# Three moves at the seam between the attention stage and the expert stage: a subtraction's source, six transposes, three gate instructions

## The chip, the cores and the metric

The kernel runs on one core of one Trainium2 chip. Its time is the device time of one execution in microseconds; less is better. Times of single instructions come from one profiled execution, whose span runs from the first to the last instruction.

## The reference

Three layers run one after the other, all in float32:

```python
for t in range(S):                                  # attention: B 4, H 8, S 768, D 48
    state = alpha[:, :, t, :, None] * state + einsum('bhd,bhe->bhde', k[:, :, t], v[:, :, t])
    y[:, :, t] = einsum('bhd,bhde->bhe', q[:, :, t], state)
x = y.transpose(0, 2, 1, 3).reshape(B * S, H * D)   # 3072 rows of 384
do = x @ w_skip > 0                                 # experts: only rows with a positive skip score
e_idx = argmax(x @ w_gate); gate = softmax(x @ w_gate)[e_idx]
x[do] += gate * (relu(x[do] @ w1[e_idx]) @ w2[e_idx])     # 8 experts, 384 -> 1024 -> 384
h = maximum(maximum(x @ m1, x @ m2), x @ m3)        # last layer: 384 -> 768 -> 384
out = h @ m_out
```

## The kernel before, in words

**Attention.** The work is cut into 24 steps: 4 batches (`b`) of 6 chunks (`c`) of 128 positions. Step `n` computes the scores of step n+1 (`scores`, L246), the transposes of its keys (`trans`, L237), the rows of the step before (`rows`, L297: four products that turn the attention output `yt` into 128 rows of 384 plus nine routing scores, in the PSUM tile `px`), then its own output (`outs`, L284 and L287, in `py`, copied to `yt` by L290) and the state's update (`upd`, L264; L271 and L272 on VectorE and the two copies L275 and L276 into `bd`, which the next step's `outs` reads). ScalarE copies `px` to `xr` in SBUF (L311). For the last four chunks it also writes the rounded high part `xq[0]` (L310), and `low_part` (L315, VectorE) writes the low part `xq[1]`, the difference between the row and its high part. For chunks 0 and 1 of the last batch `xsplit` does the same from `xr` (L99, L100).

**Routing.** `route` is a generator that gives every row a slot of its expert (256 slots each); `stage` runs it to its next stop. For batches 0 to 2 it covers six chunks. The last batch is cut in two: `rA` (chunks 0 to 3) and `rB` (chunks 4 and 5). A route computes the expert (L339 to L358), sends the rows to the row table `x2` in HBM (L361), counts with two products (L365, L366), forms the slot number (L371 to L381) and, in the last batch, the one-hot tiles `p0` (L384). Then come the gates (L392 to L394: sum, plus 1e-9, reciprocal) and one indirect DMA from GpSimd's queue for each chunk (L397), which writes the rows with their gates into `slots` in HBM.

**The first expert's input.** Expert 0 doesn't wait for the last batch's rows to go through HBM. The tile `xe` is loaded from `slots` after the scatters of batches 0 to 2 (L512, SyncE's queue). The last batch's rows are added by products: `gather` (L522) multiplies `xq` with `p0` into three PSUM accumulators `acc`, one for each third of the 384 columns, and six transposes (L540, weights `xe`, moving operand `ident`) add the rows that came through `xe`. `split` then forms `xh` and `xl` of expert 0 (L99, L100).

**Experts.** 64 slices `s`: `gemm1(s)` (L624 to L626) and, two slices later, `gemm2` (L642 to L644). The input of expert 1 is loaded with `xload(1)` (L599) once all scatters have landed, and TensorE transposes it from slice 5 on (`xprep`, L612). After the experts the last layer runs 36 groups of products (L778 to L780, L810 to L812).

**What sets the order.** The kernel is recorded with a manual schedule: each engine runs its instructions in the order in which the code issues them, and semaphores hold an instruction until its inputs are there. An instruction that waits holds everything behind it on its engine.

Of the kernel before, what the change touches and what calls it, by code (L numbers as in the profile page):

```python
# [9 lines left out]
F32 = mybir.dt.float32  # L10
# [5 lines left out]
ALU = mybir.AluOpType  # L16
# [4 lines left out]
NP = H // 2  # L21
C = 128
NC = S // C
PR = 128
# [6 lines left out]
DM = H * D  # L31
# [3 lines left out]
CAP = 256  # L35
# [28 lines left out]
def tile_gla_moe_moe2(ctx, tc, akq, vp, rp, wgt, cst, io, ew, md, out):  # L64
    nc = tc.nc
    V, A, G, T, SY = nc.vector, nc.scalar, nc.gpsimd, nc.tensor, nc.sync
# [6 lines left out]
    k3, nf1, nf2 = DM // 128, FF // 128, FF2 // 128  # L73
# [24 lines left out]
    def split(h, l, src, eng=None):  # L98
        A.copy(h, src)  # L99
        (eng or V).tensor_tensor(l, src, h.bitcast(F32), ALU.subtract)  # L100

    with tc.manual_schedule():
        cs = const.tile([128, 3 * 128 + NTILE + 8], F32, name="cs")
        rps = const.tile([PR, NP, 105], F32, name="rps")
        ident = cs[:, 0:128]
# [14 lines left out]
        xq = []  # L120
# [12 lines left out]
        ps_s = pool("ps_s", 1, space=PSUM)  # L133
        ps_k = pool("ps_k", 1, space=PSUM)
        ps_u = pool("ps_u", 1, space=PSUM)
# [28 lines left out]
        def warm(n):  # L164
            pw = ps_r.tile([128, 512], F32, name="pr")
            for i in range(n):
                T.matmul(pw, ones, wu, start=True, stop=True)
# [4 lines left out]
        nseq = len(seq)  # L172
# [13 lines left out]
        def vload(j):  # L186
            if j >= nseq:
                return
            b, c = seq[j]
            vt[j] = hp.tile([128, VW], F32, name="vt")  # L190
            SY.dma_start(out=vt[j], in_=vp[b, :, c])
# [32 lines left out]
        def prep(j):  # L224
            if j < nseq:
                sf = suffixes(j)
                inverse(j, sf)
                prefixes(j, sf)

        fr, kks, yts, wt, xr, lg = {}, {}, {}, {}, {}, {}  # L230

        def trans(j):
            if seq[j][1] == NC - 1:
                return
            pk = ps_k.tile([128, NP, PR], F32, name="pk")
            for p in range(NP):
                T.transpose(pk[:, p, :], kh[j][:, p, :], ident)  # L237
            kks[j] = wk.tile([128, NP, PR], F32, name="kk")
            A.copy(kks[j], pk)

        def scores(j):
            ps = [ps_s.tile([128, NP, C], F32, name=f"ps{i}") for i in range(2)]
            for p in range(NP):
                for i in range(2):
                    r0 = 64 * i
                    T.matmul(ps[i][:, p, :], kh[j][r0:r0 + 64, p, :], qh[j][r0:r0 + 64, p, :],  # L246
                             start=True, stop=True)
            fr[j] = ps

        def mask(j, i):  # L250
            t = wk.tile([128, NP, C], F32, name=f"sm{i}")
            V.tensor_tensor(t, fr[j][i], cmask[:, None, :].to_broadcast([128, NP, C]), ALU.mult)
            fr[j][i] = t
# [24 lines left out]
        def outs(j):  # L278
            c = seq[j][1]
            sm = fr.pop(j)  # L280
            py = ps_y.tile([PR, NP, C], F32, name="py")
            if c:
                for p in range(NP):
                    T.matmul(py[:, p, :], bd[c % 2][:, p, :], qh[j][:, p, :], start=(p == 0), stop=False)  # L284
            for p in range(NP):
                for i in range(2):
                    T.matmul(py[64 * i:64 * i + 64, p, :], vt[j][:, (2 * p + i) * D:(2 * p + i) * D + 64], sm[i][:, p, :],  # L287
                             start=(c == 0), stop=(c == 0 or p == NP - 1))
            yts[j] = wk.tile([PR, NP, C], F32, name="yt")
            A.copy(yts[j], py)  # L290

        def rows(j):
            b, c = seq[j]
            yt = yts.pop(j)
            px = ps_x.tile([128, NP, 105], F32, name="px")
            for p in range(NP):
                T.matmul(px[:, p, :], yt[:, p, :], rps[:, p, :], start=True, stop=True)  # L297
            if c == 0:
                xr[b] = wk.tile([128, NC, XW], F32, name="xr")
                lg[b] = cols[f"lg{b % 2}"].rearrange("p (c e) -> p c e", c=NC)  # L300
            pairs = lambda t: t.rearrange("p (a d) -> p a d", a=NP)
            direct = b == B - 1 and c > 1

            def logits():
                V.tensor_reduce(lg[b][:, c, :], px[:, :, 96:105].rearrange("p a e -> p e a"), AX.X, ALU.add)

            if direct:
                if c == NC - 1:
                    logits()
                A.copy(pairs(xq[0][:, c]), px[:, :, 0:96])  # L310
            A.copy(pairs(xr[b][:, c, 0:DM]), px[:, :, 0:96])  # L311
            if not direct or c < NC - 1:
                logits()
            def low_part():
                V.tensor_tensor(pairs(xq[1][:, c]), px[:, :, 0:96], pairs(xq[0][:, c]).bitcast(F32), ALU.subtract)  # L315

            return low_part

# [132 lines left out]
        def stage(*gs):  # L451

            gs = list(gs)
            while gs:
                gs = [g for g in gs if next(g, 1) == 0]

        def step_routes():
            for r in routes:
                stage(r)

        def xsplit(c0, c1, eng=None):
            z = slice(c0, c1)
            split(xq[0][:, z], xq[1][:, z], xr[B - 1][:, z, 0:DM], eng)

        scores(0)
        trans(0)
        prep(1)
# [2 lines left out]
        for n, (b, c) in enumerate(seq):  # L470
            pre = [n + 2] if n == 0 else [n + 2, n + 3] if n == 1 else [n + 3]
            pre = [j for j in pre if j < nseq]
            if n + 1 < nseq:
                scores(n + 1)
                trans(n + 1)
            for j in pre:
                prep(j)
            if n + 1 < nseq:
                mask(n + 1, 0)
                mask(n + 1, 1)  # L480
            low_part = rows(n - 1) if n else None
            outs(n)
            upd(n)
            if n > nseq - 4:
                low_part()
            vload(n + 5)
            if n and seq[n - 1][1] == NC - 1:
                routes.append(route(b - 1, 0, NC))
            step_routes()
            if n < 2:  # L490
                warm(KEEP[n])
            if n == 3:
                patterns()
            if n == 10:
                SY.dma_start(out=iota, in_=io)
            if 3 <= n < 7:
                for i in range((n - 3) * NSLOT // 512, (n - 2) * NSLOT // 512):
                    SY.dma_start(out=slots[i * 128:(i + 1) * 128, :], in_=zt)
            if 7 <= n < 11:
                wpart(n - 7)  # L500
            if n in (11, 12, 13, 18):
                wsplit(min(n - 11, 3), G)
            if n in (17, 18):
                wload(n - 16)
            if n == nseq - 4:
                rs.close()
                xep = xes.enter_context(tc.tile_pool(name="xep", bufs=1, side="right"))
                xq += [xep.tile([128, NC, DM], F32R, name=f"xq{i}") for i in range(2)]
                p0 = xep.tile([128, NC, CAP], F32R, name="p0")
                xe = xep.tile([128, 2, DM], F32, name="xe")  # L510
            if n == nseq - 3:
                SY.dma_start(out=xe, in_=slots[0:CAP, 0:DM].rearrange("(m p) d -> p m d", p=128))  # L512
            if n == nseq - 2:
                rA = route(B - 1, 0, 4)
                stage(rA)
                xsplit(0, 2)

        def gather(c0, c1):
            for c in range(c0, c1):
                for k in range(k3):  # L520
                    for t in xq:
                        T.matmul(acc[k], t[:, c, k * 128:(k + 1) * 128], p0[:, c], start=(c == 0 and t is xq[0]),  # L522
                                 stop=(c == NC - 1 and t is xq[1]))

        stage(rA)
        stage(rA)
        low_part = rows(nseq - 1)
        rB = route(B - 1, 4, NC)
        stage(rB)
        low_part()  # L530
        acc = [ps_k.tile([128, NP, PR], F32, name="pk").rearrange("p a b -> p (a b)")[:, 0:CAP],
               ps_u.tile([128, 512], F32, name="pu")[:, 0:CAP],
               ps_s.tile([128, NP, C], F32, name="ps0").rearrange("p a b -> p (a b)")[:, 0:CAP]]
        gather(0, 3)
        stage(rB)
        stage(rA)
        gather(3, 4)
        for k in range(k3):
            for m in range(2):
                T.matmul(acc[k][:, m * 128:(m + 1) * 128], xe[:, m, k * 128:(k + 1) * 128], ident,  # L540
                         start=False, stop=False)
        stage(rB)
        gather(4, NC)
        stage(rB)
        xs_, xh_, xl_, ix_ = {}, {}, {}, {}
        xh_[0] = xhp.tile([128, k3, CAP], F32R, name="xh")
# [493 lines left out]
```

## Time and profile before

| | |
|---|---|
| median of 3 runs | 614.12 us (614.08 to 615.0) |
| the profiled execution's own time | 614.44 us |
| its span, first to last instruction | 612.6 us |
| time around the span | 1.84 us |
| TensorE busy | 585.9 us, 96% |
| VectorE, ScalarE, GpSimd busy | 359.8, 239.7, 161.7 us |
| mean granted TensorE clock | 0.994 of 2.4 GHz |

The attention stage runs up to about 139 us, the seam between the stages from there to 146 us, the experts to about 303 us, the last layer to the end. TensorE is the engine that is nearly always busy, so the rows to look for are those in which it waits. In a timeline a row has the start, the duration, the engine, the line, the operation, the tile written and the tile read, the shape, how many instructions were merged into the row, and in brackets how long the engine was idle before it and what ended that. PE is TensorE's matmul, PEld its weight load, DVE is VectorE, ACT ScalarE, POOL GpSimd, SPq the DMA queue of SyncE.

### The profile page before, as it was taken

What the parts mean: (1) busy time and instruction counts of PE and PEld (TensorE: products, weight loads), DVE (VectorE), ACT (ScalarE), POOL (GpSimd) and SP (SyncE); (2) the same over time, 40 slices, a digit from 0 to 9 for tenths busy, and PEclk for the clock granted to TensorE, in tenths of its full rate; (3) what the DMA queues carried; (4) which work ended last, traced back from release to release, by engine and by line L of the source; (5) the groups of instructions that cost most, each with busy time, mean ns of one, the idle gap of its engine ahead of it and who ended that gap; (6) DMA issues with size and microseconds to landing.
All of it is one profiled execution on the core that took longest, in us unless ns stands there. A gap on an engine that the chain in (4) does not pass through costs nothing.

```text
span 612.6 us, 10428 instructions
## 1 busy us (share of the span) xinstructions
PE 585.9 (96%) x4103; PEld 525.8 (86%) x4103; DVE 359.8 (59%) x630; ACT 239.7 (39%) x495; POOL 161.7 (26%) x142
## 2 busy tenths in 40 slices
PE   5999999989999999999999999999999999999994
PEld 3888888889998999999888888888888888888884
DVE  5899999966889899998577223222322322332222
ACT  2555575654666666654333121121121212112111
POOL 5544598744256455455100000000000000000000
PEclk9999999999999999999999999999999999999998
DMA  8789998925777767673241030020003001001001
GB/s 326 263 236 340 294 309 304 364 63 184 256 281 250 244 230 259 231 282 121 73 169 38 1 103 1 1 99 6 0 1 103 1 1 51 1 0 52 0 2 57
DMA packets 29243, 85.67 MB, mean 140 GB/s; under 512 B 3298, under 2 KB 20688, under 8 KB 27264
## 3 DMA queue, kind: packets, MB, share of 16 engines
q1 hardware_dynamic: 26336, 79.68, 37.7%
q0 software_dynamic: 2560, 4.83, 2.1%
q8 instruction: 34, 0.56, 0.4%
q10 hardware_dynamic: 288, 0.39, 0.2%
q14 instruction: 25, 0.20, 0.1%
HBM read 67.47 MB, written 20.49 MB: 144 GB/s over the span
## 4 chain that ended last, share of the span: by engine, by line


## 5 line engine op out<-in xcount | busy, mean ns | idle before, releaser
L795 DVE TENSOR_TENSOR h<-ph,h 128x512 f32<-128x512 f32 x72 | 49.8, 691 | 157.8 <-PE ph L780 157.4
L778 PE MATMUL ph<-xh,mh 128*128 128x512 f32 x270 | 106.3, 394 | 0.0
L780 PE MATMUL ph<-xh,ml 128*128 128x512 f32 x270 | 105.6, 391 | 0.0
L779 PE MATMUL ph<-xl,mh 128*128 128x512 f32 x270 | 105.4, 390 | 0.0
L99 ACT CAST hh<-h 128x512 fp32r<-128x512 f32 x36 | 22.3, 620 | 143.2 <-DVE h L795 143.2
L100 POOL TENSOR_TENSOR wl<-raw,wh 128x768 fp32r<-128x768 f32 x26 | 50.4, 1938 | 57.2 <-ACT wh L99 54.5
L100 DVE TENSOR_TENSOR wl<-raw,wh 128x768 fp32r<-128x768 f32 x38 | 58.0, 1526 | 11.2 <-ACT wh L99 11.2
L99 ACT CAST wh<-raw 128x768 fp32r<-128x768 f32 x64 | 53.4, 834 | 20.8 <-PE po L644 16.6
L780 PEld LDWEIGHTS ph<-xh,ml 128*128 128x128 f32 x270 | 50.7, 188 | 10.9
L779 PEld LDWEIGHTS ph<-xl,mh 128*128 128x128 f32 x270 | 50.7, 188 | 9.9
L778 PEld LDWEIGHTS ph<-xh,mh 128*128 128x128 f32 x270 | 50.7, 188 | 9.8
L624 PE MATMUL ph<-xh,wh 128*128 128x256 f32 x192 | 56.4, 294 | 1.5 <-DVE hl L630 1.5
L625 PE MATMUL ph<-xl,wh 128*128 128x256 f32 x192 | 54.4, 283 | 0.4 <-DVE xl L100 0.3
L626 PE MATMUL ph<-xh,wl 128*128 128x256 f32 x192 | 54.3, 283 | 0.0
L812 PE MATMUL po<-mh,hl 128*128 128x384 f32 x144 | 48.6, 338 | 0.0
L810 PE MATMUL po<-mh,hh 128*128 128x384 f32 x144 | 48.4, 336 | 0.0
L811 PE MATMUL po<-ml,hh 128*128 128x384 f32 x144 | 48.4, 336 | 0.0
L793 ACT COPY h<-ph 128x512 f32<-128x512 f32 x36 | 21.1, 586 | 68.0 <-PE ph L780 68.0
L644 PE MATMUL po<-wh,hl 128*128 128x384 f32 x128 | 43.6, 340 | 1.7 <-DVE hl L630 1.3
L642 PE MATMUL po<-wh,hh 128*128 128x384 f32 x128 | 43.5, 340 | 0.0
L643 PE MATMUL po<-wl,hh 128*128 128x384 f32 x128 | 43.1, 337 | 0.0
L246 PE MATMUL ps<-q,k 64*128 64x128 f32 x384 | 31.9, 287 | 11.0 <-POOL q L221 7.1
(188 smaller groups left out, 1188.2 us busy)
## 6 DMA issues: line engine op xcount, KB each, us to landing
raw<-in_ew_dram SPq DMA_DIRECT2D x15, 1536.0 KB, 6.4
akq<-in_akq_dram SPq DMA_DIRECT2D x23, 772.5 KB, 7.0
rm<-in_md_dram SPq DMA_DIRECT2D x12, 768.0 KB, 7.7
vt<-in_vp_dram SPq DMA_DIRECT2D x24, 200.0 KB, 7.2
out_dram<-o SPq DMA_DIRECT2D x22, 192.0 KB, 2.0
xg<-x SPq DMA_DIRECT2D x5, 768.0 KB, 5.3
x<-xr SPq DMA_DIRECT2D x3, 1152.0 KB, 10.1
slots<-zt SPq DMA_DIRECT2D x16, 193.0 KB, 7.3
```

Of the source, the lines that this page charges most:

```text
L99: A.copy(h, src)
L100: (eng or V).tensor_tensor(l, src, h.bitcast(F32), ALU.subtract)
L624: T.matmul(ph, wh[:, z], xh_[e][:, k, :], start=(k == 0), stop=False)
L625: T.matmul(ph, wh[:, z], xl_[e][:, k, :], start=False, stop=False)
L626: T.matmul(ph, wl[:, z], xh_[e][:, k, :], start=False, stop=(k == k3 - 1))
L778: T.matmul(phs[w], mh[w][:, z], xh_[g][:, k, :], start=(k == 0), stop=False)
L779: T.matmul(phs[w], mh[w][:, z], xl_[g][:, k, :], start=False, stop=False)
L780: T.matmul(phs[w], ml[w][:, z], xh_[g][:, k, :], start=False, stop=(k == k3 - 1))
L795: V.tensor_tensor(n, ph, t, ALU.max)
L810: T.matmul(po, hh[:, zm], mh[3][:, z], start=(f == 0), stop=False)
L811: T.matmul(po, hh[:, zm], ml[3][:, z], start=False, stop=False)
L812: T.matmul(po, hl[:, zm], mh[3][:, z], start=False, stop=(f == nf2 - 1))
```

## The change

Three edits.

1. `low_part` reads the row from its copy `xr` in SBUF and no longer from the PSUM tile `px`.
2. The six transposes of `xe` now open the accumulators. The two for the first third stand in the last step of the loop, ahead of `rows(n - 1)`; the four others stand behind the first part's counting products. `gather` no longer starts an accumulation.
3. The third `stage(rA)` (gates and scatters of the first part) moves from between the two gathers to behind the last one, just ahead of the last `stage(rB)`.

```diff
             def low_part():
-                V.tensor_tensor(pairs(xq[1][:, c]), px[:, :, 0:96], pairs(xq[0][:, c]).bitcast(F32), ALU.subtract)
+                V.tensor_tensor(xq[1][:, c], xr[b][:, c, 0:DM], xq[0][:, c].bitcast(F32), ALU.subtract)
...
+        def xe_sums(k):
+            for m in range(2):
+                T.matmul(acc[k][:, m * 128:(m + 1) * 128], xe[:, m, k * 128:(k + 1) * 128], ident,
+                         start=(m == 0), stop=False)
...
+            if n == nseq - 1:
+                acc = [ps_k.tile([128, NP, PR], F32, name="pk").rearrange("p a b -> p (a b)")[:, 0:CAP]]
+                xe_sums(0)
             low_part = rows(n - 1) if n else None
             outs(n)
             upd(n)
...
-                        T.matmul(acc[k], t[:, c, k * 128:(k + 1) * 128], p0[:, c], start=(c == 0 and t is xq[0]),
+                        T.matmul(acc[k], t[:, c, k * 128:(k + 1) * 128], p0[:, c], start=False,
                                  stop=(c == NC - 1 and t is xq[1]))
 
+        acc += [ps_u.tile([128, 512], F32, name="pu")[:, 0:CAP],
+                ps_s.tile([128, NP, C], F32, name="ps0").rearrange("p a b -> p (a b)")[:, 0:CAP]]
         stage(rA)
+        for k in (1, 2):
+            xe_sums(k)
         stage(rA)
         low_part = rows(nseq - 1)
         rB = route(B - 1, 4, NC)
         stage(rB)
         low_part()
-        acc = [ps_k.tile([128, NP, PR], F32, name="pk").rearrange("p a b -> p (a b)")[:, 0:CAP],
-               ps_u.tile([128, 512], F32, name="pu")[:, 0:CAP],
-               ps_s.tile([128, NP, C], F32, name="ps0").rearrange("p a b -> p (a b)")[:, 0:CAP]]
         gather(0, 3)
         stage(rB)
-        stage(rA)
         gather(3, 4)
-        for k in range(k3):
-            for m in range(2):
-                T.matmul(acc[k][:, m * 128:(m + 1) * 128], xe[:, m, k * 128:(k + 1) * 128], ident,
-                         start=False, stop=False)
         stage(rB)
         gather(4, NC)
+        stage(rA)
         stage(rB)
```

On TensorE, at the loop's last step: the update of step 22 (L264), then `rows(22)` (L297) and the output of step 23 (L284). L467 is the changed kernel's line of the transposes of `xe`.

```order
 L287 MATMUL py<-sm_1919,vt 64x128
 L264 MATMUL pu<-vt,kk 64x48 x8
+L467 MATMUL pk<-cs,xe 128x128 x2
 L297 MATMUL px<-rps,yt 128x105 x4
 L284 MATMUL py<-q_1816,bd_138 128x128 x4
```

Two transposes that read `xe` now stand ahead of the products of `rows(22)`.

On TensorE, behind the loop: the first part's second counting product (L366) and the products of the last chunk's rows, `rows(23)` (L297).

```order
 L366 LDWEIGHTS ones
 L366 MATMUL pr<-ec_2020,ones 128x32
+L467 MATMUL pu<-cs,xe 128x128 x2
+L467 MATMUL ps_2062<-cs,xe 128x128 x2
 L297 MATMUL px<-rps,yt 128x105 x4
```

The other four transposes came in between; all six stood between the third and the last part of the gather before.

On VectorE, behind the last low part: the slot numbers and one-hot tiles of the second part (L371 to L384, `om_2099` and `om_2090` are the same tile in the two kernels) and the gates of the first part (L392 to L394, four chunks, so 128x4).

```order
+L371 TENSOR_TENSOR rk<-pr,om_2099 128x16
+L373 TENSOR_REDUCE pcs<-rk 128x2
+L375 SCALAR_TENSOR_TENSOR vl<-pcs,sk 128x2
+L377 SCALAR_TENSOR_TENSOR pcs<-mi,pcs 128x2
+L379 SCALAR_TENSOR_TENSOR s_2142<-vl,pcs 128x2
+L381 TENSOR_SCALAR si<-s_2142 128x2
+L384 TENSOR_SCALAR p_1898<-iota,s_2142 128x256 x2
 L392 TENSOR_REDUCE sme<-ex 128x4
 L393 TENSOR_SCALAR s_2018<-sme 128x4
 L394 RECIPROCAL xr<-s_2018 128x4
-L371 TENSOR_TENSOR rk<-pr,om_2090 128x16
```

The second part's chain now goes ahead of the first part's gates. The order of the DMAs on SyncE's queue and on GpSimd's is the same in both kernels.

## Rows read from the trace of the kernel before

**Rows 1.** The page's first part: busy time, share of span, count, by engine.

```profile
PE 585.9 (96%) x4103; PEld 525.8 (86%) x4103; DVE 359.8 (59%) x630; ACT 239.7 (39%) x495; POOL 161.7 (26%) x142
```

**Rows 2.** Busy time by stage, one stretch of the last layer; then clock, DMA.

```profile
300.00:450.00 150.00, 150.00 (x721) 129.35 (x720) 58.41 (x83) 35.08 (x61) 1.97 (x2) 1.00 0.13 45
```

**Rows 3.** Timeline of TensorE, last steps of attention.

```profile
129.82 1.11 PE L297 MATMUL px<-rps,yt 128*128 128x105 f32 x8 [0.32 <-DVE xq L315]
...
132.70 0.62 PE L264 MATMUL pu<-vt,kk 128*64 128x48 f32 x16
134.74 1.11 PE L297 MATMUL px<-rps,yt 128*128 128x105 f32 x8 [1.42 <-DVE mx L339]
...
138.52 1.14 PE L297 MATMUL px<-rps,yt 128*128 128x105 f32 x8 [0.59 <-ACT yt L290]
```

**Rows 4.** Timeline of VectorE and ScalarE, same stretch.

```profile
129.13 0.55 DVE L315 TENSOR_TENSOR xq<-px,xq 128x384 fp32r<-128x384 f32 x1
...
134.04 0.55 DVE L315 TENSOR_TENSOR xq<-px,xq 128x384 fp32r<-128x384 f32 x1
...
134.59 0.35 ACT L276 COPY bd<-w 64x192 f32<-64x192 f32 x1
```

**Rows 5.** Timeline of SyncE's queue: issues of DMAs.

```profile
135.69 0.38 SPq L512 DMA_DIRECT2D xe<-slots  x1
136.12 5.50 SPq L361 DMA_DIRECT2D x<-xr  x2
...
152.52 0.88 SPq L599 DMA_DIRECT2D xs<-slots  x2
```

**Rows 6.** Waits of SyncE's queue, 130 to 157 us: total, times, longest.

```profile
SPq L512 <- DMA slots<-xr,si: 18.8, 1, 18.8
```

**Rows 7.** Landing: all eight `xs` loads, then two writes of 130 to 165 us.

```profile
DMA to landing us min/median/max: 3.4/8.0/8.1
...
x<-xr SPq DMA_DIRECT2D x1, 768.0 KB, 5.2
...
x<-xr SPq DMA_DIRECT2D x1, 384.0 KB, 2.7
```

**Rows 8.** Timeline of VectorE at the seam.

```profile
140.14 0.19 DVE L305 TENSOR_REDUCE pcs<-px 128x9 f32<-128x36 f32 x1
...
141.90 0.53 DVE L315 TENSOR_TENSOR xq<-px,xq 128x384 fp32r<-128x384 f32 x1
...
142.76 0.18 DVE L394 RECIPROCAL xr<-s 128x4 f32<-128x4 f32 x1
142.86 0.14 DVE L371 TENSOR_TENSOR rk<-pr,om 128x16 f32<-128x16 f32 x1
...
143.89 0.61 DVE L384 TENSOR_SCALAR p<-iota,s 128x256 fp32r<-128x256 f32 x2
```

**Rows 9.** Timeline of TensorE at the seam; then its weight loads.

```profile
142.85 0.61 PE L540 MATMUL pk<-cs,xe 128*128 128x128 f32 x4
...
145.98 0.38 PE L624 MATMUL ph<-xh,wh 128*128 128x256 f32 x1
...
156.92 0.32 PEld L612 LDWEIGHTS pt<-cs,xs 128*128 128x128 f32 x2
```

**Rows 10.** Timeline of GpSimd: first scatter of the last batch.

```profile
143.70 0.97 POOL L397 DMA_INDIRECT slots<-xr,si  x1 [9.58 <-DVE s L379]
```

**Rows 11.** TensorE's restart and last matmul; windows with the granted clock (third from last).

```profile
13.49 1.33 PE L246 MATMUL ps<-q,k 64*128 64x128 f32 x16 [4.10 <-POOL q L221]
...
14.00:14.50 0.50, 0.50 (x12) 0.50 (x10) 0.50 (x1) 0.00 (x0) 0.00 (x0) 0.85 1.13 443
...
17.50:18.00 0.50, 0.50 (x18) 0.50 (x14) 0.00 (x0) 0.18 (x1) 0.00 (x0) 0.74 0.91 371
...
604.05 0.34 PE L812 MATMUL po<-mh,hl 128*128 128x384 f32 x1
...
608.25:608.50 0.25, 0.00 (x0) 0.00 (x0) 0.00 (x0) 0.00 (x0) 0.00 (x0) 0.54 0.00 0
```

## The prediction, made before the changed kernel had run

> **What bounds the kernel now.** I read the page's busy times first: TensorE is busy for 585.9 of 612.6 us, VectorE for 359.8 [rows 1]. The windows by stage say where the rest is: in the last layer TensorE is busy for 150.00 of 150.00 us [rows 2]. So what delays TensorE ahead of the experts is not given back later: whatever the seam gains or loses goes one for one into the time, unless a later wait swallows it.
>
> Then the timeline of TensorE around the change, for the waits. Three stand there [rows 3]: 0.32 us ahead of the rows of step 21 (129.82), 1.42 us ahead of those of step 22 (134.74), 0.59 us ahead of those of step 23 (138.52). The first two end when the low part has read `px`: it runs until 129.68 and until 134.59 [rows 4]. These are what the first edit is after. Next I looked at what each moved instruction reads, and when that is there. The transposes read `xe`. SyncE's queue issues this load at 135.69 [rows 5], after a wait of 18.8 us for the scatters of the batch before [rows 6]. Before the change nobody waits for `xe`, since its first reader runs at 142.85 [rows 9], 7 us later. That is the row that decides this forecast.
>
> **The change part by part**
>
> **1. Low part from SBUF.** The same 128x384 subtraction, about 0.5 us on VectorE either way. It takes TensorE's wait for `px` away: step 21's rows start 0.3 us earlier. Step 22's would too, by up to 1.4 us, but the next edit puts something ahead of them.
>
> **2. Transposes ahead of the rows of step 22.** TensorE ends the update of step 22 at 133.32 [rows 3], with the 0.3 us gained at about 133.0. The next instruction is now a weight load from `xe`. Nothing in the change moves the load of `xe` forward: SyncE's order is the same, and what it waits for (the scatters of batch 2) lies upstream of every edit. So `xe` is issued at 135.69 again. When it lands the trace doesn't say, since nobody waited for it. Nearest row: the loads `xs` from the same table with the same form and size, fastest 3.4 us [rows 7]. Bounds: 2.7 us, the 384 KB write to the row table, and 5.2 us, the 768 KB write that follows `xe` in the same queue [rows 7]. I take 3.4: `xe` is there at 139.09, and TensorE has stood still for 6.1 us. Behind it in TensorE's queue stand the rows of step 22, the output of step 23, the counting products and the rows of step 23; VectorE, ScalarE and GpSimd wait for these in turn. The two transposes take 0.61 us [rows 9], so the rows of step 22 start at 139.70 and not at 134.74: **+4.96 us**, between +4.3 and +6.8.
>
> The four other transposes stand where TensorE waited 0.59 us for `yt` [rows 3]. They take 1.22 us, so the rows of step 23 may slip by up to 0.63 us against the step before. Before the change VectorE read these rows only at 140.14 [rows 8], 0.48 us after the products' end at 139.66, because it was busy with the one-hot tiles. That covers most of it: **+0.1 us**, between 0 and 0.63. Taking the six out of the gather gives nothing: the gather's last part waits for the one-hot tiles (143.89 and on [rows 8]), and the transposes stood in that wait.
>
> **3. Gates behind.** At the seam's end VectorE's chain decides: low part until 142.43, then the first part's gates until 142.94, then L371 at 142.86 (it overlaps) up to the one-hot tiles and the gather's last part [rows 8]. With the gates out of the way L371 can start at 142.4 on this clock: **-0.45 us**, between -0.5 and 0 (it also needs the counting products). The experts' first product (145.98 before [rows 9]) then comes 4.96 + 0.1 - 0.45 = 4.6 us later.
>
> The gates have someone waiting, however: GpSimd's scatters. Before, the gates ended at 142.94 and the first scatter ran at 143.70 [rows 8, 10], so the gates were done 3.0 us ahead of the experts' first product. Now they come after the one-hot tiles, which end at 144.50 [rows 8], 1.5 us ahead of that product, and take 0.5 us more: 1.0 us ahead of it. Measured from the experts' start the whole chain slips by 2.05 us: six scatters, the wait for their landing, the load of expert 1's rows. This load was issued at 152.52 [rows 5] and by the 3.4 us landed at 155.9; TensorE first needs it at 156.92 [rows 9]. Slack 1.0 us, slip 2.05 us: TensorE waits **+1.05 us** at slice 5, between 0 and 2.05.
>
> **4. The clock.** The trace shows TensorE's clock fall twice. At the start TensorE is idle for 4.10 us until 13.49, the clock falls within 14.00 to 14.50 and is back only within 17.50 to 18.00 [rows 11], about 4.3 us after the restart. At the end the last matmul ends at 604.39 and the clock falls within 608.25 to 608.50 [rows 11], 3.9 us later. The idle stretch that edit 2 makes is 6.1 us, longer than both. So I expect the fall to 1.2 GHz while TensorE waits, and work at half speed for about the same 4.3 us after `xe` is there, where TensorE has back-to-back products. That costs half of it: **+2.1 us**, between 0 (no fall) and 4.3 (twice as long).
>
> The Trainium skill states the rule behind this in "TensorE: Matmul & The Clock Gate", section "HAM oscillation — how this bites in real kernels": a wait for a DMA between bursts of matmuls puts the array back to its low clock, and the next burst starts cold. By that rule the sum holds the 2.1 us, without it it doesn't; the trace agrees where TensorE idled for 4.10 us at the start.
>
> **Sum.** 4.6 + 1.05 + 2.1 = 7.75 us. Against the profiled execution's 614.44 us (span 612.6 and 1.84 around it) that is 622.2; the median of the runs lies 0.3 us below the profiled one: **621.9 us**.
>
> **The rivals**
>
> **A. The clock stays up, or comes back at once.** For it: the fall at the end of the trace came 3.9 us after the last matmul, so only the last 2.2 us of the wait would be at low clock, and the restart may lift it earlier than at the program's start. Against it: at the start it stayed low for 3.4 us under back-to-back work. Time: 614.12 + 4.6 + 1.05 = 619.8.
>
> **B. The load of expert 1's rows is still in time.** For it: the slack of 1.0 us rests on a landing time, not on a wait that was seen. Against it: the slip comes from VectorE's order alone. Time: 620.8.
>
> **C. `xe` lands with the row-table write that shares its queue.** The 768 KB write is issued 0.4 us behind it, and both move at the same time; 5.2 instead of 3.4 us adds 1.8. For it: the sizes of both must pass the same engines. Against it: `xe` is first in the queue, and the 3.4 us were measured with an equal load right behind. Time: 623.7.
>
> **D. TensorE doesn't wait for `xe`: the other side.** Then the first edit's gain comes through. The rows of step 22 would run from about 133.6, the output of step 23 as soon as `bd` is copied (134.94 less 0.3 [rows 4]), about 1.0 us earlier than now; with the 0.45 of edit 3 the experts start 1.4 us earlier. The late scatters then take 1.05 back at slice 5. Time: 613.7, or 612.7 if rival B holds as well. It decides if `xe` lands before 133.0. That is 2.7 us before it was issued, so the issue would have to move forward by about 6 us, and the scatter that it waits for with it. No row speaks for that.
>
> **How the numbers follow.** Forecast 0.53, A 0.20, B 0.10, C 0.12, D 0.05. The predicted time is the forecast's, 621.9. The range goes from 618.4 (no clock loss, next to no wait at slice 5, `xe` in 3.2 us) to 624.8 (C with a clock loss of 3 us). Within 0.2% means 1.2 us, about what a measurement of this kernel tells from no change. Only D is not slower: with 613.7 it is no change, with 612.7 faster. So faster 0.03, same 0.03, slower 0.94.
>
> **What would show it.** TensorE's timeline: an idle stretch of about 6 us ahead of L467, ended by the DMA of `xe`, at about 139; the rows of step 22 right behind it. The granted clock in windows from 137 to 144: near 0.5 in some of them. L371 right behind the last low part. The first scatter of the last batch some 6.5 us later than 143.70 and more by what the clock costs, and a wait of L612's weight load for `xs` of about 1 us. The forecast is wrong if L467 shows no idle time ahead of it, or if the experts' first product comes less than 4 us later.

## The result and the profile after

The changed kernel takes 620.88 us (median of 6 runs, 617.71 to 622.12) against 614.04 us for the kernel before (611.85 to 615.0 in 6 runs): a ratio of 1.0119, with a 95% interval of 1.01 to 1.0137. It is slower, by 6.8 us between the medians and 7.3 us by the ratio. The profiled execution took 620.93 us, with a span of 619.1 us, 6.5 us more than before.

The page's first part, the line that answers to [rows 1], and the window of the last layer, the line that answers to [rows 2]:

```profile
PE 588.4 (95%) x4103; PEld 527.5 (85%) x4103; DVE 361.6 (58%) x630; ACT 239.5 (39%) x495; POOL 162.3 (26%) x142
...
300.00:450.00 150.00, 149.83 (x721) 128.55 (x720) 61.32 (x89) 37.00 (x64) 1.97 (x2) 1.00 0.14 49
```

The number of instructions is the same, and TensorE is still busy for all of the last layer. So the 6.5 us lie ahead of it. The timeline of TensorE in the changed kernel, the stretch of [rows 3] and [rows 9] (L467 are the transposes of `xe`, L530 the gather, L629 the experts' first product, L617 the transposes of a later expert's rows):

```profile
131.18 0.62 PE L264 MATMUL pu<-vt,kk 128*64 128x48 f32 x16
138.52 1.19 PE L467 MATMUL pk<-cs,xe 128*128 128x128 f32 x4 [6.72 <-DMA xe<-slots]
139.51 1.88 PE L297 MATMUL px<-rps,yt 128*128 128x105 f32 x8
...
143.78 0.69 PE L467 MATMUL pu<-cs,xe 128*128 128x128 f32 x4
144.31 0.61 PE L467 MATMUL ps<-cs,xe 128*128 128x128 f32 x4
144.75 1.04 PE L297 MATMUL px<-rps,yt 128*128 128x105 f32 x8
...
149.82 0.50 PE L530 MATMUL pk<-p,xq 128*128 128x256 f32 x2 [0.80 <-DVE p L384]
...
151.49 0.38 PE L629 MATMUL ph<-xh,wh 128*128 128x256 f32 x1
...
163.74 0.41 PE L617 MATMUL pt<-cs,xs 128*128 128x128 f32 x2 [0.96 <-DMA xs<-slots]
```

The waits of 1.42 and 0.59 us ahead of the rows of steps 22 and 23 are gone. In their place stands one of 6.72 us, ended by the DMA of `xe`, and a second one of 0.96 us for `xs`. The experts' first product starts 5.51 us later than before (151.49 against 145.98), and with the 0.96 us that is the whole growth of the span. The queue of SyncE, which answers to [rows 5]:

```profile
134.76 0.38 SPq L520 DMA_DIRECT2D xe<-slots  x1
135.19 12.42 SPq L361 DMA_DIRECT2D x<-xr  x2
...
160.21 0.87 SPq L604 DMA_DIRECT2D xs<-slots  x2
```

The load of `xe` is issued 3.0 us after TensorE has ended its last product ahead of L467 (131.80), and the transposes can start 3.8 us after the issue. Windows of the changed kernel, the third column from the end being the granted clock (1.00 is 2.4 GHz, 0.50 is 1.2 GHz):

```profile
135.50:136.00 0.50, 0.00 (x0) 0.00 (x0) 0.13 (x1) 0.00 (x0) 0.00 (x0) 0.50 0.67 40
...
138.50:139.00 0.50, 0.48 (x2) 0.50 (x3) 0.00 (x0) 0.00 (x0) 0.00 (x0) 0.50 1.08 409
...
142.00:142.50 0.50, 0.50 (x6) 0.50 (x4) 0.19 (x2) 0.28 (x1) 0.00 (x0) 0.77 0.00 0
142.50:143.00 0.50, 0.50 (x9) 0.38 (x9) 0.47 (x2) 0.00 (x0) 0.00 (x0) 1.00 0.00 0
```

TensorE is idle in the first of them and the clock is already down. It comes back within 142.0 to 142.5, some 3.7 us after the restart. The eight products of L297 at 139.51 take 1.88 us, at 144.75 they take 1.04. Last, VectorE and GpSimd at the seam, the rows that answer to [rows 8] and [rows 10]:

```profile
147.90 0.53 DVE L315 TENSOR_TENSOR xq<-xr,xq 128x384 fp32r<-128x384 f32 x1
148.35 0.17 DVE L371 TENSOR_TENSOR rk<-pr,om 128x16 f32<-128x16 f32 x1
149.42 0.61 DVE L384 TENSOR_SCALAR p<-iota,s 128x256 fp32r<-128x256 f32 x2
...
150.36 0.18 DVE L394 RECIPROCAL xr<-s 128x4 f32<-128x4 f32 x1
```

```profile
151.29 0.97 POOL L397 DMA_INDIRECT slots<-xr,si  x1 [18.11 <-DVE xr L394]
```

L371 now stands right behind the last low part, and the gates' last instruction, L394, behind the one-hot tiles. GpSimd's first scatter of the last batch comes at 151.29, only 0.2 us ahead of the experts' first product; before it was 2.3 us ahead.

The two executions do not run level ahead of the change. The rows of step 20 (L297) start at 124.98 before (first line) and at 123.82 here (second line):

```profile
124.98 1.04 PE L297 MATMUL px<-rps,yt 128*128 128x105 f32 x8
123.82 1.04 PE L297 MATMUL px<-rps,yt 128*128 128x105 f32 x8
```

That is 1.16 us earlier; in the runs below they start between 122.17 and 125.98, so this varies. Below I measure distances from these rows, or between rows of one trace.

### The profile page after: what moved, and what is told of

It reads as the page before. It is cut to its first block, busy times and chain, and to the rows that moved or that the text cites. A ratio compares the mean times of both kernels' runs of the same rounds, so it can differ in the third digit from the quotient of the medians.

```text
span 619.1 us, 10430 instructions
## 1 busy us (share of the span) xinstructions
PE 588.4 (95%) x4103; PEld 527.5 (85%) x4103; DVE 361.6 (58%) x630; ACT 239.5 (39%) x495; POOL 162.3 (26%) x142
## 4 chain that ended last, share of the span: by engine, by line
## 5 line engine op out<-in xcount | busy, mean ns | idle before, releaser
L100 DVE TENSOR_TENSOR wl<-raw,wh 128x768 fp32r<-128x768 f32 x38 | 59.6, 1568 | 9.9 <-ACT wh L99 9.9
L629 PE MATMUL ph<-xh,wh 128*128 128x256 f32 x192 | 56.4, 294 | 1.5 <-DVE hl L635 1.5
```

What stands on the lines that cost most here:

```text
L629: T.matmul(ph, wh[:, z], xh_[e][:, k, :], start=(k == 0), stop=False)
```

## The experiments

**Theory.** The loss is edit 2: TensorE waits for a load that the change does not move, and comes out of the wait at 1.2 GHz. Edits 1 and 3 are small. **Rivals:** the low parts or the gates carry part of it; the low clock costs nothing that shows in the time; TensorE would not wait if the load were there, and the loss would stay.

The four sets of runs below were made on four chips. Each ratio is against the kernel before on the same chip. On the first and the fourth that kernel takes 618.5 and 618.7 us, on the second and third 612.9 and 613.8; the last section comes to this. "By the ratio" means the ratio's distance from 1 times the time of the kernel before; it can differ by up to about 1 us from the difference of the medians.

### Each edit alone, first chip

Edit 1 alone, `e1_low_part_alone`: the changed kernel with the transposes and the gates where they were before.

```
-        def xe_sums(k):
...
-                xe_sums(0)
...
+        stage(rA)
         gather(3, 4)
+        for k in range(k3):
+            for m in range(2):
...
-        stage(rA)
```

> The kernel before with edit 1 alone (low part from its SBUF copy). Theory (the wait of the rows' products for the low part is all that this edit touches): the 0.32 us and most of the 1.42 us ahead of the rows of steps 21 and 22 go; the output of step 23 is then held by the copies of bd, so the experts start about 1.0 us earlier: 613.0 to 613.4 us against 614.0. Rival (VectorE's chain at the seam hides it): 614.0, no change.

Edit 2 alone, `e2_transposes_alone`: the changed kernel with the low part read from `px` and the gates at their old place.

```
-                V.tensor_tensor(xq[1][:, c], xr[b][:, c, 0:DM], xq[0][:, c].bitcast(F32), ALU.subtract)
+                V.tensor_tensor(pairs(xq[1][:, c]), px[:, :, 0:96], pairs(xq[0][:, c]).bitcast(F32), ALU.subtract)
...
+        stage(rA)
         gather(3, 4)
...
-        stage(rA)
```

> The kernel before with edit 2 alone (the transposes of xe moved forward). Theory (this edit is nearly the whole loss): TensorE waits about 5.5 to 6 us for xe, then works 3 to 4 us at the low clock; the experts start 6 to 7 us later, no wait for expert 1's rows at slice 5: 620 to 621 us. Rival (the loss is that of the gates moved behind): 614 to 615 us.

Edit 3 alone, `e3_gates_alone`: the kernel before with `stage(rA)` moved behind the last gather.

```
-        stage(rA)
         gather(3, 4)
...
         gather(4, NC)
+        stage(rA)
         stage(rB)
```

> The kernel before with edit 3 alone (gates of the first part moved to the end). Theory (0.45 us gained on VectorE's chain, 1.05 us lost at slice 5, where TensorE waits for expert 1's rows because the scatters slip by about 2 us against the experts' start): 614.6 us, between 614.2 and 615.2. Rival (the load is still in time): 613.6 us and no wait of the transposes of xs.

Measured against 618.54 us: edit 1 gave 617.38 (ratio 0.9983, 0.9971 to 0.9995), edit 2 622.55 (1.0046, 1.0031 to 1.0061), edit 3 619.65 (1.0012, 0.9999 to 1.0025). Edits 1 and 3 came out at the size expected, edit 3 with an interval that just holds no change (TensorE waits 0.96 us for `xs` in its trace, as forecast). Edit 2 missed: 2.9 us by the ratio (4.0 between the medians), where 6 to 7 were expected. TensorE's timeline in that run shows a shorter wait:

```profile
133.34 1.11 PE L297 MATMUL px<-rps,yt 128*128 128x105 f32 x8 [2.85 <-DVE w L272]
...
141.88 1.19 PE L467 MATMUL pk<-cs,xe 128*128 128x128 f32 x4 [3.44 <-DMA xe<-slots]
142.86 1.88 PE L297 MATMUL px<-rps,yt 128*128 128x105 f32 x8
```

On this chip TensorE has already lost 2.85 us to VectorE one step earlier, and the clock is down behind this wait too. Against the same kernel on the third chip (below), and counted from the rows of step 20, TensorE comes 4.1 us later to a load that is there 1.4 us later, and so it waits 3.44 us for it and not 6.20. In the run of edit 3, which has the transposes at their old place, the rows of step 22 start 13.90 us behind those of step 20, here 16.88: 2.98 us later, where the changed kernel has 5.93 against the kernel before. Behind these rows this execution loses another 2.66 us up to the experts' first product, at the low clock and with the gates in the way; at 624.91 us it is the slowest of its nine, so its rows show why the wait is shorter and not what the median lost. The wait is as long as TensorE is early, and its price holds only for a chip that runs the stretch ahead at the same pace.

### Edits 1 and 2 alone, and the whole change again, third chip

The same three kernels where the kernel before takes 613.75 us, without new edits: `f4_low_part_alone_again`, `f3_transposes_alone_again`, and the changed kernel itself, `f1_changed_again`.

> Edit 1 alone once more, beside the others. Theory: about 1.0 us faster than the kernel before, rows of step 22 held by the output's copy and the next output by bd. Rival (the last low part's late place is what made the seventh run faster, since it had edit 1 as well): no more than 0.4 us faster.

> Edit 2 alone once more, beside the changed kernel. Theory: the wait for xe is 0.3 us shorter than in the changed kernel, no wait at slice 5, the gates 0.45 us in the way: within 1 us of the changed kernel, so the whole loss is edit 2's. Rival (the other two edits carry part of it): more than 2 us faster than the changed kernel.

> The changed kernel itself once more, beside the next three on one chip. Theory: 6 to 9 us slower than the kernel before where TensorE reaches xe 6 to 7 us ahead of its landing; on a chip where TensorE is held up earlier in the last steps (3.4 us of wait for xe, as in the first run of the transposes alone) only 3 to 4 us slower.

Measured: edit 1 alone 612.75 us (0.9987, 0.9973 to 1.0001), edit 2 alone 620.45 (1.011, 1.0091 to 1.013), the whole change 621.38 (1.0115, 1.0095 to 1.0135). By itself edit 2 loses 6.8 us by the ratio, 0.3 less than the whole, which is within the intervals. So the rival that the other two edits carry 2 us or more of it falls. TensorE's timeline with edit 2 alone:

```profile
137.12 1.19 PE L467 MATMUL pk<-cs,xe 128*128 128x128 f32 x4 [6.20 <-DMA xe<-slots]
138.10 1.88 PE L297 MATMUL px<-rps,yt 128*128 128x105 f32 x8
...
143.34 1.04 PE L297 MATMUL px<-rps,yt 128*128 128x105 f32 x8
...
148.88 0.50 PE L530 MATMUL pk<-p,xq 128*128 128x256 f32 x2 [1.29 <-DVE p L384]
...
150.56 0.39 PE L629 MATMUL ph<-xh,wh 128*128 128x256 f32 x1
```

and with edit 1 alone:

```profile
133.34 1.14 PE L297 MATMUL px<-rps,yt 128*128 128x105 f32 x8 [0.29 <-ACT yt L290]
134.72 1.16 PE L284 MATMUL py<-q,bd 128*128 128x128 f32 x8 [0.24 <-ACT bd L276]
```

Edit 1 does what it is for: the wait of 1.42 us of [rows 3] is down to 0.29 and 0.24 us, and the experts' first product comes 20.28 us behind the rows of step 20 (125.08 to 145.36), before 21.00 (124.98 to 145.98). By the time it is 0.8 us on this chip, with an interval that holds both the 1.0 us expected and no change. In the changed kernel this gain cannot show, since TensorE waits for `xe` in the same place: 6.20 us without edit 1, 6.72 and 6.78 with it. Some 0.35 us of this are TensorE's earlier arrival. The other 0.2 are a later load, and they are a small price of edit 1 itself. In all ten profiles of kernels with this edit, the scatter of GpSimd that starts 0.2 us behind the first low part takes 1.17 to 1.21 us, in the four without it 0.97 or 0.98; the scatters are what the load of `xe` waits for. The third scatter of batch 2, before and in the changed kernel:

```profile
129.31 0.97 POOL L397 DMA_INDIRECT slots<-xr,si  x1 [0.30 <-issue]
128.17 1.19 POOL L397 DMA_INDIRECT slots<-xr,si  x1 [0.32 <-issue]
```

The first low part runs from 129.13 there [rows 4] and from 127.97 here. Why the scatter takes longer beside a low part that reads SBUF, no run here shows.

### The load of `xe` early, second chip

`e5_xe_early`: the changed kernel, with `xe` filled from a table that no scatter writes, so that the load is issued at 121.60, ahead of the rows of step 20. It leaves out the rows that expert 0 gets through `slots`.

```
-                SY.dma_start(out=xe, in_=slots[0:CAP, 0:DM].rearrange("(m p) d -> p m d", p=128))
+                SY.dma_start(out=xe, in_=ew[0, :, 0:2 * DM].rearrange("p (m d) -> p m d", m=2))
```

> The changed kernel with xe loaded from the first expert's weights in HBM instead of from the slots, so that the load needn't wait for the scatters (expert 0's input is then without the rows of batches 0 to 2). Theory (the wait for xe and the low clock after it are the loss; what is left of the change is the gain of edits 1 and 3 less the wait at slice 5): no wait ahead of the first transposes, clock 1.00, 613.3 to 613.9 us. Rival (the transposes' new places or the open accumulators cost by themselves): 616 us or more without a wait for xe.

Measured: 612.84 us against 612.87, ratio 1.0002 (0.9986 to 1.0017). A gain of 0.1 to 0.7 us was expected and none is seen; the interval, 0.9 us below to 1.0 above, holds both. TensorE's timeline:

```profile
130.70 0.62 PE L264 MATMUL pu<-vt,kk 128*64 128x48 f32 x16
131.25 0.71 PE L467 MATMUL pk<-cs,xe 128*128 128x128 f32 x4
131.80 1.04 PE L297 MATMUL px<-rps,yt 128*128 128x105 f32 x8
...
155.37 0.41 PE L617 MATMUL pt<-cs,xs 128*128 128x128 f32 x2 [0.93 <-DMA xs<-slots]
```

No wait ahead of L467, no low clock (1.00 all through the seam), and the loss is gone, to within the interval. In this trace the experts' first product comes 19.80 us behind the rows of step 20 (123.35 to 143.15), before 21.00: 1.20 us are gained, and 0.93 of them are lost again at L617. So the wait and what it does to the clock are the loss, and the place of the transposes by itself is none that shows.

### Gates back, second chip

`e6_gates_back`: the changed kernel with the gates where they were, so edits 1 and 2.

```
+        stage(rA)
         gather(3, 4)
...
-        stage(rA)
```

> The changed kernel with the gates back in their old place (edits 1 and 2 alone). Theory (edit 3 costs 1.05 at slice 5 and gains 0.45): no wait of the transposes of xs, L371 0.45 us later behind the gates, 620.0 to 620.5 us against 620.9. Rival (edit 3 is a gain): 621.3 us.

Measured: 621.91 us, ratio 1.0138 (1.0114 to 1.0161). The 0.6 us do not show in the time. The timeline has them: TensorE no longer waits at L617, and from the rows of step 23 to the experts' first product it takes 7.24 us (146.31 to 153.55), in the changed kernel 6.74 (144.75 to 151.49), so the gates on VectorE's chain cost 0.5 us. But in this execution the clock stayed low longer, as its windows show (L467 starts at 139.06):

```profile
144.00:145.00 1.00, 1.00 (x14) 1.00 (x12) 0.00 (x0) 0.00 (x0) 0.00 (x0) 0.52 0.00 0
145.00:146.00 1.00, 1.00 (x14) 0.83 (x11) 0.40 (x3) 0.56 (x1) 0.00 (x0) 1.00 0.00 0
```

That is 5.9 us at 1.2 GHz and not 3.7. The 0.5 us of this edit is smaller than the difference that the clock makes from one execution to the next; this run doesn't decide it by its time.

### The clock kept up: first, third and fourth chip

Products of a zero tile stand in TensorE's queue ahead of the first transposes, so that it has work while `xe` is on its way: 26 in `e4_clock_kept` and `g1_clock_kept_26`, 20 in `f2_clock_kept_shorter`.

```
                 acc = [ps_k.tile([128, NP, PR], F32, name="pk").rearrange("p a b -> p (a b)")[:, 0:CAP]]
+                warm(26)
                 xe_sums(0)
```

> The changed kernel with 26 more products of zeros (bf16, 128x512, into the free counting bank) ahead of the first transposes of xe, so that TensorE works through most of its wait; they should end about 1 us before xe lands. Theory (low clock after the wait costs about 1.9 us of the loss): granted clock 1.00 at the seam, 618.7 to 619.3 us against 620.9, and less spread between runs. Rival (the products at low clock lie beside other waits and cost nothing): 620.5 to 621 us at a clock of 1.00.

> The changed kernel with 20 instead of 26 products of zeros ahead of the first transposes of xe (20 x 0.22 = 4.5 us), which end before xe lands where the wait is 6.7 us. Theory (low clock after the wait costs 1.5 to 3 us): granted clock 1.00 at the seam, 1.5 to 3 us faster than the changed kernel on the same chip. Rival (the low clock costs nothing): the same time at a clock of 1.00. Where the wait for xe is under 4.5 us the products themselves hold TensorE up and the run tells nothing.

> The changed kernel with 26 products of a zero tile in TensorE's queue ahead of the first two transposes of xe. With 20 of them they ended 2.4 us before xe was there and the clock still fell; at 0.22 us each the six more end about 1.1 us before it, so that TensorE is hardly ever idle while xe is on its way. Theory (the loss is the wait for xe and beside it about 2 us of work at 1.2 GHz): the rows of step 22 start at the same distance behind the issue of xe as in the changed kernel, the granted clock stays at 1.00 between the wait and the gather, and the kernel before stands 5.0 to 5.7 us ahead and not 7 to 7.6 (ratio 1.008 to 1.0095). Rival (the low clock costs nothing that isn't hidden behind VectorE's chain): ratio 1.0115 as for the changed kernel. Second rival (the products themselves end after xe has landed and delay the transposes): the rows of step 22 start later than in the changed kernel, and the time says nothing of the clock.

Measured: 26 products gave 621.99 us on the first chip (1.0053, 1.0032 to 1.0074) and 622.18 on the fourth (1.0051, 1.0031 to 1.007); 20 gave 619.98 on the third (1.0099, 1.0079 to 1.0118), 1.0 us by the ratio under the whole change there, with intervals that overlap. None of the three times decides it, and the times expected of the two runs with 26 products were missed, the last as its second rival has it. On the first and fourth chip TensorE came late, and the products delayed the transposes: the rows of step 22 start 6.27 us behind the issue of `xe` on the fourth (135.78 to 142.05), 4.75 in the changed kernel. On the third they ended 2.4 us early, and the clock fell all the same:

```profile
138.82 1.19 PE L467 MATMUL pk<-cs,xe 128*128 128x128 f32 x4 [2.40 <-DMA xe<-slots]
139.81 1.88 PE L297 MATMUL px<-rps,yt 128*128 128x105 f32 x8
...
146.31 1.04 PE L297 MATMUL px<-rps,yt 128*128 128x105 f32 x8
...
153.06 0.39 PE L630 MATMUL ph<-xh,wh 128*128 128x256 f32 x1
```

What the three do give is the price, as a distance within a trace. With 26 products the clock stood at 1.00 throughout; the timeline on the fourth chip:

```profile
135.99 5.79 PE L167 MATMUL pr<-wu,ones 128*128 128x512 bf16 x26
141.61 0.61 PE L467 MATMUL pk<-cs,xe 128*128 128x128 f32 x4
142.05 1.04 PE L297 MATMUL px<-rps,yt 128*128 128x105 f32 x8
145.02 0.69 PE L467 MATMUL pu<-cs,xe 128*128 128x128 f32 x4
...
146.00 1.04 PE L297 MATMUL px<-rps,yt 128*128 128x105 f32 x8
...
152.74 0.39 PE L630 MATMUL ph<-xh,wh 128*128 128x256 f32 x1
```

The instructions from the first transpose to the experts are those of the changed kernel in the same order. From L467 to the experts' first product they take 11.13 us here (141.61 to 152.74), and the same 11.13 on the first chip. In the changed kernel it is 12.97 us (138.52 to 151.49), in its second profile 13.85 (139.77 to 153.62), with 20 products 14.24 (138.82 to 153.06). So the low clock costs 1.8, 2.7 and 3.1 us in these three executions, all of it ahead of the rows of step 23: from there to the experts it is 6.74 or 6.75 us in all of them. From L467 to the rows of step 23 it is 4.39 us at 1.00 (141.61 to 146.00); the three runs that keep the gates in their old place have 6.22 (edit 2 alone, third chip), 7.25 (gates back) and 7.47 (edit 2 alone, first chip), so 1.8, 2.9 and 3.1 us there.

### A version that beats both, second chip

`e7_low_part_late`: edit 1 alone, and the last low part behind the last one-hot tiles.

```
         stage(rB)
-        low_part()
...
         gather(0, 3)
...
         stage(rB)
+        low_part()
         gather(4, NC)
```

> The kernel before with edit 1, and the last chunk's low part moved behind the one-hot tiles of the second part (transposes and gates in their old places). It should beat both kernels: edit 1's gain of about 1.0 us, and VectorE's chain at the seam loses the last subtraction, 0.45 us: 612.5 to 613.0 us. Rival (the last products then wait for this low part): 613.0 to 613.4, as edit 1 alone.

Measured: 611.22 us (610.28 to 613.99) against 612.87, ratio 0.9978 (0.9962 to 0.9994), 1.3 us faster than before. TensorE's timeline:

```profile
134.74 1.14 PE L297 MATMUL px<-rps,yt 128*128 128x105 f32 x8 [0.59 <-ACT yt L290]
...
140.22 0.61 PE L539 MATMUL ps<-cs,xe 128*128 128x128 f32 x4
140.59 0.48 PE L522 MATMUL pk<-p,xq 128*128 128x256 f32 x2
...
142.25 0.39 PE L624 MATMUL ph<-xh,wh 128*128 128x256 f32 x1
```

From the rows of step 23 to the experts it takes 7.51 us, with edit 1 alone 7.72 (137.64 to 145.36), so the later low part gives 0.2 us in one profile each; the rest is edit 1, and the intervals of the two overlap. The changed kernel waits 0.80 us for the last one-hot tiles; here, as before the change, the transposes of `xe` fill the time until these are there, and no wait is seen. Of their 1.3 us (139.33 to 140.59) about 0.3 are left as a cost: the gather goes on 0.68 us behind the start of the last one-hot tiles (L384, 139.91), 0.40 in the changed kernel.

## Why the prediction held, step by step

The terms below are distances in the profiled executions, before [rows 3, 9] and after, with the clock's part taken out by the runs that kept it at 1.00. The forecast had the mechanism right, and its sizes nearly so.

| step | predicted us | measured us |
|---|---|---|
| rows of step 22 later, at full clock | 4.96 | 5.38 |
| four other transposes | 0.1 | 0.17 |
| seam's end, VectorE's chain | -0.45 | -0.72 |
| wait for `xs` | 1.05 | 0.96 |
| low clock | 2.1 | 1.84 |
| sum | 7.75 | 7.63 |

- **The wait for `xe`.** It is where and as long as forecast, 6.72 us against 6.1. From the rows of step 20 to those of step 22 it was 9.76 us before and 15.69 after, 5.93 more; 0.55 of it is the clock (L467 to L297 0.99 us, at 1.00 0.44). The remaining 0.42 over the forecast: the load was issued 0.23 us later behind step 20, and TensorE started 3.8 us after its issue (3.7 to 3.8 in four more profiles, 4.4 on the first chip) where the sum had 3.4 from the fastest `xs` [rows 7]; the two transposes took 0.44 and not 0.61, since the next row starts before the last has ended. The forecast let the issue stay where it was, since the scatters lie upstream of every edit; but one of them runs beside the first low part and took 0.2 us longer. And the fastest `xs` was not the best row: the three issued between 130 and 165 us in the kernel before land in 3.8 us in the median. Rival C (5.2 us) fell: the write behind `xe` in the queue is on its way at the same time (the 1.18 MB of both move between 135 and 140 us), and the load was not 1.8 us late. Rival D fell with the first row.
- **The low clock.** From the rows of step 22 to those of step 23 it was 3.78 us before, 5.24 after, 3.95 with the clock at 1.00. So rival A fell: the clock costs 1.84 us in this execution, near the 2.1 taken. It was worked out from a stretch of 4.3 us, and 3.7 were measured. At the program's start, however, the clock fell only some 0.9 us behind the restart [rows 11], so 3.4 of those 4.3 us were at half speed, and the wait there was for GpSimd and not for a DMA: a near row and not the same case. The Trainium skill, "TensorE: Matmul & The Clock Gate", section "HAM oscillation — how this bites in real kernels", has it that products behind a DMA wait start on a cold array; the trace agrees, with 0.50 in the windows behind the wait. The size did not hold over executions: 1.8 to 3.1 us.
- **The gates.** VectorE's chain got shorter and GpSimd's later, as forecast. The chain's gain is 0.72 us against the kernel before, 0.5 against the same kernel with the gates back. The 0.23 beyond the gates is the rows of step 23 starting that much later, behind the four transposes: 1.00 us behind the second counting product (143.75 to 144.75), before 0.77 (137.75 to 138.52), while VectorE's one-hot tiles start 1.34 us behind it in both (145.09 and 139.09). So the four transposes cost nothing in the end, and the table's second and third line hold the same 0.2 us with opposite signs. The wait for `xs` came at slice 5 with 0.96 us, 0.85 in the second profile, and is gone with the gates back. So rival B fell too.
- **The low part.** The forecast gave it no gain of its own in the changed kernel, and it has none there, but the 0.2 us of the later load; alone it gives 1.1 us on the first chip and 0.8 on the third by the ratio, there with an interval that just holds no change.

From the same rows: the sum fits within 0.12 us, while the steps err by up to 0.4 us in both directions. That closeness is partly luck, since the low clock cost 2.7 us in the second profile of the same kernel. The range's upper end, 624.8, comes to 624.6 when its terms are added up; nothing rests on it. The span grew by only 6.5 us, since this execution was 1.16 us earlier ahead of the change. Of the median's 620.88 against 621.9, I cannot say more than that the runs of this kernel spread over 4.4 us.

## What to carry to other kernels

Before you move the reader of a DMA's data forward, find the row that issues that DMA and add a measured landing time: a load that nobody waits for shows no wait, and says nothing on whether it would be in time ten microseconds earlier. Work that stands in a wait costs nothing there, and taking it out gains only if what the wait was for comes earlier as well. In this kernel a wait of 6.2 to 6.8 us on TensorE brought 1.8 to 2.9 us of low clock with it, and this part differed from one execution to the next.

## What the runs showed of the hardware

- **How long the clock stays low behind a wait varies.** Under back-to-back products it came back 3.7 us after the restart in the first profile of the changed kernel and with edit 2 alone on the third chip, 5.6 in its second, 5.9 with the gates back, and 6.5 with 20 zero products and with edit 2 alone on the first chip. The times of the changed kernel go with it roughly: 617.71 us at a mean clock of 0.991, 619.64 to 621.46 at 0.987 or 0.988, 622.12 at 0.985.
- **The clock fell with TensorE idle for 2.4 us** behind 4.3 us of products on a zero tile (f2). With 26 products and no idle time behind them it stayed at 1.00. A wait of 1.97 or 1.98 us in step 22 had both outcomes: in the run of edit 1 alone on the first chip the clock fell just behind it, at about 132.4, and was back at 135.7; in the two runs with 26 products it stayed at 1.00 behind the same wait, which comes ahead of these products.
- **A scatter of GpSimd that starts 0.2 us behind a VectorE subtraction took 0.2 us longer where the subtraction reads SBUF**: 1.17 to 1.21 us in ten profiles, 0.97 or 0.98 in the four where it reads PSUM. A scatter that was under way when the next low part started took 0.97 in the changed kernel too.
- **On two of the four chips VectorE and ScalarE stand still around step 22**, in all five profiles there and in no other. VectorE waits 3.7 us ahead of L271, where it waits 1.3 in the kernel before, and it is for this that TensorE waits 2.85 us, or 1.98 with edit 1 in the kernel; then both engines wait once more, for about 3 us. The second waits of edit 1 alone on the first chip (engine, line, releaser, total, times, longest):

```profile
DVE sm L252 <- remote: 3.1, 1, 3.1
ACT xq L310 <- remote: 2.9, 1, 2.9
```

Behind the first wait the clock went down to 0.50 in three of the five, from 134.7 to 138.1 with edit 2 alone, ahead of anything that this edit moves. The same kernel before takes 618.5 us on the one and 618.7 on the other, 612.9 to 614.0 elsewhere, and a loss that is a wait of TensorE comes out smaller, 2.9 and not 6.8 us by the ratio for edit 2. What these engines wait for the profile doesn't name, and no run here was made to find it.
